# Normalising attention results in SBUF instead of fetching them back from DRAM

## The chip, the cores and the metric

The kernel runs on one core of a Trainium2 chip. The metric is the device time of one execution in microseconds (us). Five engines matter: TensorE (PE in the profile, with its weight loads as PEld), VectorE (DVE), ScalarE (ACT), GpSimd (POOL) and SyncE (SP), whose queue issues all of this kernel's transfers. The transfers themselves are carried by 16 DMA engines.

## The reference

Capped softmax attention, then two feed-forward blocks, all in float32 (the weights come as float64 words):

```python
B, H, S, D = 4, 12, 448, 64                       # q, k, v: (B, H, S, D)
scores = cap * np.tanh(q @ k.T / np.sqrt(D) / cap)
attn = np.exp(scores - scores.max(-1))
attn = attn / (attn.sum(-1) + 1e-09)
x = (attn @ v)        # reordered to 1792 tokens x 768
h = np.maximum(x @ w_in, 0.0)                     # 768 -> 2048
x = h * h @ w_out                                 # 2048 -> 768
gate = 1.0 / (1.0 + np.exp(-(x @ w_gate)))        # 768 -> 1536
return (gate * (x @ w_val)) @ w_out2              # 1536 -> 768
```

## The kernel before

**Tiling.** Two heads form a pair; there are 24 pairs (4 batches of 6), numbered n. The attention of a pair has four steps of 128 keys (the last one takes the 64 left of both heads at once). `scores` multiplies k by q, `softmax` applies tanh and exp on ACT, `pv` multiplies by v and accumulates in one PSUM tile "pv", of which there is one. Each v is stored beside 64 columns of ones, so that the result has, for head j of the pair, 64 rows of values and 64 rows that all hold the sum of the exponentials: for head 0 values in rows 0 to 63 and sums in 64 to 127, for head 1 the other way round. The first 12 pairs (`early`, batches 0 and 1) use float32 products; the other 12 split the operands in a high and a low part and take three products.

**Feed-forward.** The tokens are worked on in two passes: tokens 0 to 767 (blocks of 256 and 512), then 768 to 1791 (two blocks of 512). Every product there is taken three times, with high and low parts. A weight tile of the first pass is loaded as 64-bit words (`load_w`, line 480), converted on ACT and DVE (`convert`, lines 497 to 507), stored as float32 for the second pass (`keep`), and split (`round_w`, ACT and POOL). There are two tiles of words, two "raw" tiles and four split ones; a raw tile is free when its store has landed. The first pass has 82 weight tiles: 16 of w1, 24 of w2, 24 of the gate and its value, 18 of wo.

**Order of the work.** `Flow` plays the kernel through in the program's own model of time while it is built: jobs are generators that take a buffer (`"take"`), put an instruction into an engine's queue with a rank (lower goes first), or wait for a landing that `flow.landing` estimates. The order so found is fixed, and every engine then takes its instructions in that order, waiting where one isn't ready. `pick` writes PE's order: first the early pairs (the lead-in: scores of pair n between the products by v of pair n - 1), then the units of pass one, with the steps of the late pairs spread between them (`ATT`, `gap`), then pass two. The first units of pass one read all 768 features of a token, so the 256-token block needs pairs 0 to 5 and the 512-token block needs pairs 0 to 11.

**The stage that is changed.** `result` takes a pair from the end of its last `pv` step to x. Line 382 (early, DVE) or 384 (late, ACT) copies the PSUM tile into `xe`, one of 11 tiles "pt" of 128 x 2 x 448; the exponentials use the same tiles, and those of step 3 use three tiles "th" of 128 x 448. Line 390 stores 65 rows of each head (values and one row of sums) in DRAM, `xd`. Line 396 loads the two rows of sums as 16 rows of 56 (`sg`, by `dma`, line 222), lines 397 and 398 add eps and take the reciprocal on 16 partitions, line 399 stores the 896 reciprocals in `rd` (line 222 again). Line 410 fetches the values back from `xd`, 128 rows, and line 411 loads `rd` repeated over 64 rows for each head:

```python
y = xd[b][p].rearrange("(j r) s -> j r s", j=2)[:, 1:D + 1]
nc.sync.dma_start(out=xt[:, 0], in_=y)
nc.sync.dma_start(out=xt[:, 1], in_=rd[b][p].unsqueeze(1).to_broadcast((2, D, S)))
```

The target `xt` is a tile "acc" of the feed-forward part for early pairs and a tile "pt" for late ones. Line 415 multiplies on DVE, and `normalize` splits x in a high and a low part, which stay in SBUF (tokens below 768) or go to DRAM for pass two (`store_x`).

Of the kernel before, what the change touches and what calls it, by code (L numbers as in the profile page):

```python
# [10 lines left out]
F32 = mybir.dt.float32  # L11
# [3 lines left out]
ALU = mybir.AluOpType  # L15
ENGINES = mybir.EngineType

B, H, S, D = 4, 12, 448, 64
KC = 4
SP = 512  # L20
NP = H // 2
P = 128
DM = H * D
CC = DM // P
# [3 lines left out]
QK = S + SP  # L28
ALIGN = 256

PT, TH, WB = 11, 3, 4
# [122 lines left out]
def attn_mlp_kernel(ctx: ExitStack, tc: tile.TileContext, qk, v, cap, w1, w2, wg, wv, wo, out):  # L154
    nc = tc.nc
# [4 lines left out]
    dr = ctx.enter_context(tc.tile_pool(name="dr", bufs=1, space=bass.MemoryType.DRAM))  # L160
# [11 lines left out]
    def T(pool, tag, shape, dt=F32, bufs=1):  # L172
        pool = wp if pool == "wp" else open_pools[pool][1]
        return pool.tile(shape, dt, tag=tag, name=tag, bufs=bufs, align_bytes=ALIGN)

    def f32(ap):
        return ap.bitcast(F32)
# [8 lines left out]
    eps = const.tile([P, 1], F32, name="eps")  # L186
# [9 lines left out]
    def bank2(tag, pool=ps):  # L196
        return pool.tile([P, 2, 512], F32, tag=tag, name=tag, bufs=1)

    flow = Flow({
        "acc0": CC, "r0": 3, "g0": 2, "gx0": FG, "xa0": CC, "acc1": CC, "r1": 3, "g1": 2, "gx1": FG, "xa1": CC,  # L200
        "w64": 2, "raw": 2, "wh": WB, "pn": 0, "sb": 3, "pvb": 1, "v": 2, "qkh": 2, "pt": PT, "th": TH, "sg": 2,
        "qk": 2, "vr": 1})
# [5 lines left out]
    def on(engine, length, write, rank=1):  # L208
        return "on", engine, length, write, rank

    def act(out, in_, func=AF.Copy, rank=1, extra=0.0, **kw):
        return on("ACT", flow.act(cols(out)) + extra, lambda: nc.scalar.activation(out=out, in_=in_, func=func, **kw), rank)  # L212

    def sub(out, a, b, rank=1):
        return on("DVE", flow.dve(cols(out)), lambda: nc.vector.tensor_tensor(out=out, in0=a, in1=b, op=ALU.subtract), rank)  # L215

    def copy(out, in_, rank=1):
        return on("DVE", flow.dve1(cols(out)), lambda: nc.vector.tensor_copy(out, in_), rank)  # L218


    def dma(out, in_, size, store=False, rate=330e3, issue=0.42):
        yield on("SP", issue, lambda: nc.sync.dma_start(out=out, in_=in_))
        yield "for", flow.landing(size, store, rate)


# [3 lines left out]
    NV = 2  # L229
    v1, v2 = {}, {}  # L230

    XR = D + 2
    xd = [[dr.tile([2 * XR, S], F32, name=f"xd_{b}_{p}") for p in range(NP)] for b in range(B)]
    rd = [[dr.tile([2, S], F32, name=f"rd_{b}_{p}") for p in range(NP)] for b in range(B)]
    xn = [dr.tile([P, 2, WIDTH[1]], F32, name=f"xn_{p}") for p in range(NP)]
    RP, RN = 16, 2 * S // 16
# [5 lines left out]
    def early(n):  # L244
        return n < lead

    def score_tile(step, dt=F32):
        if step < 3:
            return T("att", "pt", [P, 2, S], dt, PT)
        return T("att", "th", [P, 1, S], dt, TH)  # L250
# [105 lines left out]
    def pv(n, step):  # L356
        if step == 0:
            st["o", n] = bank2("pv")
        o = st["o", n]
        ph, pl = st.pop(("p", n, step))  # L360
        c = (step + 1) % KC
        terms = [(v1, ph)] if early(n) else [(v2, ph), (v1, pl), (v1, ph)]
        for m, (vt, pt) in enumerate(terms):
            for j in range(2):

                r, u = (slice(0, P), j) if step < 3 else (slice(j * D, (j + 1) * D), 0)
                x = j if vt is v2 else 2 * j
                w = vt[n][r, c, x:x + 2, :].rearrange("p x d -> p (x d)")
                nc.tensor.matmul(  # L369
                    out=o[:, j, :S], lhsT=w, rhs=pt[r, u], start=step == 0 and m == 0, stop=step == 3 and m == len(terms) - 1)  # L370
        return result(n, step, o)

    def result(n, step, o):
        for _ in range(1 if early(n) else 2):
            flow.put("pt" if step < 3 else "th")
        if step < 3:
            return
        b, p = pairs[n]
        yield "take", "pt"
        xe = T("att", "pt", [P, 2, S], F32, PT)  # L380
        if early(n):
            yield on("DVE", 1.08, lambda: nc.vector.tensor_copy(xe, o[:, :, :S]), 0)
        else:
            yield act(xe, o[:, :, :S], rank=0)
        flow.put("pvb")
        flow.put("v")
        flow.fire(("pv", n))
        for j in range(2):
            r0, e0 = (XR, D - 1) if j else (1, 0)
            yield on("SP", 0.42, lambda: nc.sync.dma_start(out=xd[b][p][r0:r0 + D + 1], in_=xe[e0:e0 + D + 1, j]))  # L390
        yield "for", flow.landing(2 * (D + 1) * S * 4, True, 220e3)
        flow.put("pt")
        yield "take", "sg"
        sg = T("att", "sg", [RP, RN], bufs=2)
        rr = T("att", "rr", [RP, RN], bufs=2)
        yield from dma(sg, xd[b][p][XR - 1:XR + 1].rearrange("r (i s) -> (r i) s", s=RN), 0)
        yield on("DVE", 0.24, lambda: nc.vector.tensor_scalar(out=sg, in0=sg, scalar1=eps[:RP], scalar2=None, op0=ALU.add))
        yield on("DVE", 0.49, lambda: nc.vector.reciprocal(rr, sg))
        yield from dma(rd[b][p].rearrange("r (i s) -> (r i) s", s=RN), rr, 0, True)
        flow.put("sg")  # L400
        kind = "acc0" if early(n) else "pt"
        yield "take", kind
        if early(n):
            xt = T("mlp0", "acc", [P, QK], bufs=CC)[:, :2 * S].rearrange("p (x s) -> p x s", x=2)
        else:
            xt = T("att", "pt", [P, 2, S], F32, PT)
        y = xd[b][p].rearrange("(j r) s -> j r s", j=2)[:, 1:D + 1]

        def load():
            nc.sync.dma_start(out=xt[:, 0], in_=y)  # L410
            nc.sync.dma_start(out=xt[:, 1], in_=rd[b][p].unsqueeze(1).to_broadcast((2, D, S)))

        yield on("SP", 1.2, load, 0)
        yield "for", flow.landing(2 * P * S * 4, rate=170e3)
        yield on("DVE", flow.dve(S), lambda: nc.vector.tensor_tensor(out=xt[:, 0], in0=xt[:, 0], in1=xt[:, 1], op=ALU.mult), 0 if early(n) else 2)
        c0, c1 = b * S, (b + 1) * S
        for x0, x1 in ((c0, min(c1, T0)), (max(c0, T0), c1)):
            if x0 < x1:
                yield from normalize(n, x0, x1, xt[:, 0, x0 - c0:x1 - c0])
        flow.put(kind)  # L420

    def normalize(n, c0, c1, xu):
        p = pairs[n][1]
        w = c1 - c0
        if c1 <= T0:
            if ("x", 0, p) not in st:
                yield "take", "xa0"
                st["x", 0, p] = T("mlp0", "xa", [P, 2, WIDTH[0]], F32R, CC)  # L430
            dst = st["x", 0, p][:, :, c0:c1]
        else:
            yield "take", "pt"
            dst = T("att", "pt", [P, 2, S], F32R, PT)[:, :, :w]
        yield copy(dst[:, 0], xu, 0) if early(n) else act(dst[:, 0], xu, rank=2)
        yield sub(dst[:, 1], xu, f32(dst[:, 0]), 0 if early(n) else 2)
        if c1 <= T0:
            flow.fire(("x", 0, p, c1))
        else:
            flow.spawn(store_x(p, dst, c0 - T0, w))  # L440

    def store_x(p, dst, c, w):
        yield from dma(xn[p][:, :, c:c + w], f32(dst), 2 * P * w * 4, True)
        flow.put("pt")
        st["stored"] = st.get("stored", 0) + 1
        if st["stored"] == NP * 3:
            close_pool("att")
            open_pool("act1", "right")
            flow.fire("act1")
# [219 lines left out]
    for i, u in enumerate(units):  # L669
        k, kind, x = u["key"]  # L670
# [213 lines left out]
```

## Time and profile before

| | |
|---|---|
| median of 3 runs | 1340.55 us (1338.13 to 1343.11) |
| the profiled execution | 1339.74 us, span 1338.0 us from first to last instruction |
| PE busy | 1221.7 us (91%) |
| DVE busy | 645.7 us (48%) |
| ACT busy | 587.6 us (44%) |
| POOL busy | 278.8 us (21%) |
| DMA | 160.92 MB, 120 GB/s over the span |

A share over the whole span is a mean over unlike stages: the lead-in with the early pairs, pass one with the late pairs between its units, and pass two. They are better read by windows. PE's busy time holds time at a reduced clock as well: the granted clock (PEclk) is printed as a share of the full 2.4 GHz, and 0.50 is the lower level of 1.2 GHz. "Idle before" in a list in order of time is how long the engine stood still before that instruction, and behind the arrow stands what ended the wait. "SPq" rows are the issues of transfers; a transfer lands later.

### The profile page before, as it was taken

What the parts mean: (1) busy time and instruction counts of PE and PEld (TensorE: products, weight loads), DVE (VectorE), ACT (ScalarE), POOL (GpSimd) and SP (SyncE); (2) the same over time, 40 slices, a digit from 0 to 9 for tenths busy, and PEclk for the clock granted to TensorE, in tenths of its full rate; (3) what the DMA queues carried; (4) which work ended last, traced back from release to release, by engine and by line L of the source; (5) the groups of instructions that cost most, each with busy time, mean ns of one, the idle gap of its engine ahead of it and who ended that gap; (6) DMA issues with size and microseconds to landing.
All of it is one profiled execution on the core that took longest, in us unless ns stands there. A gap on an engine that the chain in (4) does not pass through costs nothing.

```text
span 1338.0 us, 15427 instructions
## 1 busy us (share of the span) xinstructions
PE 1221.7 (91%) x5880; PEld 984.8 (74%) x5880; DVE 645.7 (48%) x919; ACT 587.6 (44%) x866; POOL 278.8 (21%) x174
## 2 busy tenths in 40 slices
PE   8876737999899979988999999999999999999998
PEld 5443426888678767777778788888888888888887
DVE  3474425878688877687788520121215220122222
ACT  7664414565636665657555234424244223221220
POOL 0012001313122222122122222222222212212210
PEclk9887859999899999898999999999999999999999
DMA  5374323655555564655366751111211111111112
GB/s 170 108 221 139 122 81 121 192 176 164 181 163 180 151 191 154 187 188 162 117 177 190 254 196 52 44 54 41 64 39 56 55 32 55 56 32 58 53 33 102
DMA packets 76634, 160.92 MB, mean 120 GB/s; under 512 B 20448, under 2 KB 35088, under 8 KB 76560
## 3 DMA queue, kind: packets, MB, share of 16 engines
q1 hardware_dynamic: 76560, 159.93, 38.7%
q8 instruction: 46, 0.75, 0.2%
q14 instruction: 28, 0.23, 0.1%
HBM read 115.69 MB, written 44.21 MB: 120 GB/s over the span
## 4 chain that ended last, share of the span: by engine, by line
PE 51%; DMA 25%; DVE 13%; ACT 4%; issue 3%; SPq 2%; POOL 0%; ACTq 0%; DVEq 0%; POOLq 0%
PE pn L544 16%; PE pn L543 16%; PE pn L545 16%; DMA acc<-rd 6%; DMA pt<-rd 5%; DMA s_w<-raw 4%; DMA rd<-rr 3%; DMA s_wv<-raw 3%; DVE raw L505 2%; PE pv L369 2%; DVE raw L507 2%; DVE raw L501 2%; DMA s_wo<-raw 2%; DVE pt L215 1%; DMA xd<-pt 1%
## 5 line engine op out<-in xcount | busy, mean ns | idle before, releaser
L528 POOL TENSOR_TENSOR wl<-raw,wh 128x512 fp32r<-128x512 f32 (+1 forms) x164 | 276.0, 1684 | 1001.2 <-ACT wh L212 762.8
L543 PE MATMUL pn<-xa,wl 128*128 128x512 f32 (+1 forms) x960 | 353.0, 368 | 2.5 <-DVE g L588 1.3
L544 PE MATMUL pn<-xa,wh 128*128 128x512 f32 (+1 forms) x960 | 351.7, 366 | 0.0
L545 PE MATMUL pn<-xa,wh 128*128 128x512 f32 (+1 forms) x960 | 351.0, 366 | 0.0
L544 PE MATMUL pn<-gx,wh 128*128 128x512 f32 (+1 forms) x672 | 246.9, 367 | 4.9 <-DVE gx L215 4.8
L543 PE MATMUL pn<-gx,wl 128*128 128x512 f32 (+1 forms) x672 | 246.8, 367 | 4.8 <-ACT gx L212 4.7
L545 PE MATMUL pn<-gx,wh 128*128 128x512 f32 (+1 forms) x672 | 245.4, 365 | 0.0
L212 ACT ACTIVATE wh<-raw 128x512 fp32r<-128x512 f32 (+1 forms) x160 | 117.0, 731 | 284.6 <-PE pn L545 236.8
L543 PEld LDWEIGHTS pn<-xa,wl 128*128 128x128 f32 x960 | 183.7, 191 | 35.8 <-issue 3.9
L545 PEld LDWEIGHTS pn<-xa,wh 128*128 128x128 f32 x960 | 183.2, 191 | 29.0
L544 PEld LDWEIGHTS pn<-xa,wh 128*128 128x128 f32 x960 | 183.4, 191 | 28.8 <-DVE xa L215 0.3
L369 PE MATMUL pv<-pt,v 128*128 128x448 f32 x360 | 132.8, 503 | 77.3 <-DVE pt L218 38.5
L369 PEld LDWEIGHTS pv<-pt,v 128*128 128x128 f32 x360 | 70.9, 212 | 122.5 <-DVE pt L218 36.6
L215 DVE TENSOR_TENSOR gx<-g,gx 128x512 fp32r<-128x512 f32 (+1 forms) x112 | 83.8, 749 | 160.0 <-ACT gx L212 160.0
L543 PEld LDWEIGHTS pn<-gx,wl 128*128 128x128 f32 x672 | 128.4, 191 | 27.7 <-ACT gx L212 6.4
L544 PEld LDWEIGHTS pn<-gx,wh 128*128 128x128 f32 x672 | 128.3, 191 | 26.7 <-DVE gx L215 7.0
L545 PEld LDWEIGHTS pn<-gx,wh 128*128 128x128 f32 x672 | 128.3, 191 | 20.0
L606 DVE TENSOR_TENSOR acc<-pn,acc 128x512 f32<-128x512 f32 (+1 forms) x120 | 74.2, 620 | 122.4 <-PE pn L545 122.0
L588 DVE TENSOR_TENSOR g<-pn,r 128x512 f32<-128x512 f32 (+1 forms) x48 | 29.7, 619 | 176.5 <-PE pn L545 176.5
L212 ACT ACTIVATE raw<-w 128x512 f32<-128x512 f32 (+1 forms) x78 | 60.7, 778 | 114.4 <-DMA s_w<-raw 45.7
L212 ACT ACTIVATE gx<-g 128x512 fp32r<-128x512 f32 (+1 forms) x112 | 64.4, 575 | 68.9 <-DVE g L588 67.1
L212 ACT ACTIVATE r<-pn 128x512 f32<-128x512 f32 (+1 forms) x112 | 59.9, 535 | 69.6 <-PE pn L545 64.5
(72 smaller groups left out, 1042.5 us busy)
## 6 DMA issues: line engine op xcount, KB each, us to landing
w<-in_w_dram SPq DMA_DIRECT2D x16, 768.0 KB
w<-in_w_dram SPq DMA_DIRECT2D x24, 512.0 KB
w<-in_wg_dram SPq DMA_DIRECT2D x12, 768.0 KB
w<-in_wv_dram SPq DMA_DIRECT2D x12, 768.0 KB
w<-in_wo_dram SPq DMA_DIRECT2D x18, 512.0 KB
s_w<-raw SPq DMA_DIRECT2D x16, 384.0 KB
s_w<-raw SPq DMA_DIRECT2D x24, 256.0 KB
xa<-xn SPq DMA_DIRECT2D x12, 512.0 KB
```

What stands on the lines that cost most here:

```text
L212: return on("ACT", flow.act(cols(out)) + extra, lambda: nc.scalar.activation(out=out, in_=in_, func=func, **kw), rank)
L215: return on("DVE", flow.dve(cols(out)), lambda: nc.vector.tensor_tensor(out=out, in0=a, in1=b, op=ALU.subtract), rank)
L369: nc.tensor.matmul(out=o[:, j, :S], lhsT=w, rhs=pt[r, u], start=step == 0 and m == 0, stop=step == 3 and m == len(terms) - 1)
L501: yield on("DVE", flow.dve1(n), lambda: nc.vector.tensor_scalar(out=raw, in0=raw, scalar1=LOW, scalar2=HIGH, op0=ALU.max, op1=ALU.min))
L505: yield on("DVE", flow.dve(n), lambda: nc.vector.scalar_tensor_tensor(out=mu, in0=lo, scalar=29, in1=mu, op0=ALU.logical_shift_right, op1= ...
L507: yield on("DVE", flow.dve(n), lambda: nc.vector.scalar_tensor_tensor(out=mu, in0=hi, scalar=0xC0000000, in1=mu, op0=ALU.bitwise_and, op1= ...
L528: yield on("POOL", 0.15 + n * 0.0023, lambda: nc.gpsimd.tensor_tensor(out=lo, in0=raw, in1=f32(hi), op=ALU.subtract))
L543: nc.tensor.matmul(out=o, lhsT=wl[:, s], rhs=hi, start=i == 0, stop=False)
L544: nc.tensor.matmul(out=o, lhsT=wh[:, s], rhs=lo, start=False, stop=False)
L545: nc.tensor.matmul(out=o, lhsT=wh[:, s], rhs=hi, start=False, stop=i == n - 1)
L588: yield on("DVE", flow.dvep(w), lambda: nc.vector.tensor_tensor(out=g, in0=o, in1=st["r", k, f, off], op=ALU.mult))
L606: yield on("DVE", flow.dvep(w), lambda: nc.vector.tensor_tensor(out=acc, in0=o, in1=acc, op=ALU.add))
```

## The change

The values of a pair stay in `xe` until the reciprocals come. The DRAM tiles `xd` and both transfers to and from them are gone. Two transfers take the row of sums of each head from `xe` (one partition, 448 elements) to 8 partitions of 56 in `sg`, from SBUF to SBUF. The reciprocals still go to `rd` in DRAM and come back by two transfers, one for each head, of 64 rows each, into `bc`: a tile "acc" for early pairs, a tile "th" for late ones. Two multiplies, one for each half of the partitions, write into `xe[:, 0]`. `xe` is given back after `normalize`. The transfers, the addition and the reciprocal get rank 0, ahead of the others that are ready.

```diff
-    def dma(out, in_, size, store=False, rate=330e3, issue=0.42):
-        yield on("SP", issue, lambda: nc.sync.dma_start(out=out, in_=in_))
+    def dma(out, in_, size, store=False, rate=330e3, issue=0.42, rank=1):
+        yield on("SP", issue, lambda: nc.sync.dma_start(out=out, in_=in_), rank)
-    XR = D + 2
-    xd = [[dr.tile([2 * XR, S], F32, name=f"xd_{b}_{p}") for p in range(NP)] for b in range(B)]
-        for j in range(2):
-            r0, e0 = (XR, D - 1) if j else (1, 0)
-            yield on("SP", 0.42, lambda: nc.sync.dma_start(out=xd[b][p][r0:r0 + D + 1], in_=xe[e0:e0 + D + 1, j]))
-        yield "for", flow.landing(2 * (D + 1) * S * 4, True, 220e3)
-        flow.put("pt")
         yield "take", "sg"
         sg = T("att", "sg", [RP, RN], bufs=2)
         rr = T("att", "rr", [RP, RN], bufs=2)
-        yield from dma(sg, xd[b][p][XR - 1:XR + 1].rearrange("r (i s) -> (r i) s", s=RN), 0)
-        yield on("DVE", 0.24, lambda: nc.vector.tensor_scalar(out=sg, in0=sg, scalar1=eps[:RP], scalar2=None, op0=ALU.add))
-        yield on("DVE", 0.49, lambda: nc.vector.reciprocal(rr, sg))
-        yield from dma(rd[b][p].rearrange("r (i s) -> (r i) s", s=RN), rr, 0, True)
+        for j in range(2):
+            r0 = (1 - j) * D
+            src = xe[r0:r0 + 1, j].rearrange("o (i s) -> o i s", s=RN)
+            yield on("SP", 0.34, lambda: nc.sync.dma_start(out=sg[j * RP // 2:(j + 1) * RP // 2], in_=src), 0)
+        yield "for", flow.landing(0)
+        yield on("DVE", 0.24, lambda: nc.vector.tensor_scalar(out=sg, in0=sg, scalar1=eps[:RP], scalar2=None, op0=ALU.add), 0)
+        yield on("DVE", 0.49, lambda: nc.vector.reciprocal(rr, sg), 0)
+        yield from dma(rd[b][p].rearrange("r (i s) -> (r i) s", s=RN), rr, 0, True, rank=0)
         flow.put("sg")
-        kind = "acc0" if early(n) else "pt"
+        kind = "acc0" if early(n) else "th"
         yield "take", kind
-        if early(n):
-            xt = T("mlp0", "acc", [P, QK], bufs=CC)[:, :2 * S].rearrange("p (x s) -> p x s", x=2)
-        else:
-            xt = T("att", "pt", [P, 2, S], F32, PT)
-        y = xd[b][p].rearrange("(j r) s -> j r s", j=2)[:, 1:D + 1]
-        def load():
-            nc.sync.dma_start(out=xt[:, 0], in_=y)
-            nc.sync.dma_start(out=xt[:, 1], in_=rd[b][p].unsqueeze(1).to_broadcast((2, D, S)))
-        yield on("SP", 1.2, load, 0)
-        yield "for", flow.landing(2 * P * S * 4, rate=170e3)
-        yield on("DVE", flow.dve(S), lambda: nc.vector.tensor_tensor(out=xt[:, 0], in0=xt[:, 0], in1=xt[:, 1], op=ALU.mult), 0 if early(n) else 2)
+        bc = T("mlp0", "acc", [P, QK], bufs=CC)[:, :S] if early(n) else score_tile(3)[:, 0]
+        for j in range(2):
+            yield on("SP", 0.42, lambda: nc.sync.dma_start(
+                out=bc[j * D:(j + 1) * D], in_=rd[b][p][j].unsqueeze(0).to_broadcast((D, S))), 0)
+        yield "for", flow.landing(P * S * 4, rate=135e3)
+        xu = xe[:, 0]
+        for j in (1, 0):
+            r = slice(j * D, (j + 1) * D)
+            yield on("DVE", flow.dve(S), lambda: nc.vector.tensor_tensor(
+                out=xu[r], in0=xe[r, j], in1=bc[r], op=ALU.mult), 0 if early(n) else 2)
+        flow.put(kind)
         c0, c1 = b * S, (b + 1) * S
         for x0, x1 in ((c0, min(c1, T0)), (max(c0, T0), c1)):
             if x0 < x1:
-                yield from normalize(n, x0, x1, xt[:, 0, x0 - c0:x1 - c0])
-        flow.put(kind)
+                yield from normalize(n, x0, x1, xu[:, x0 - c0:x1 - c0])
+        flow.put("pt")
```

## Rows read from the trace of the kernel before

**Rows 1.** Busy time of each engine by stage, with granted clock and DMA share.

```profile
core 0: us, PE busy (x) PEld busy (x) DVE busy (x) ACT busy (x) POOL busy (x), PEclk, DMA share, GB/s
0.00:100.00 100.00, 78.56 (x336) 46.65 (x337) 50.03 (x72) 67.00 (x81) 5.14 (x8) 0.93 0.55 167
100.00:230.00 130.00, 82.41 (x349) 55.42 (x348) 56.76 (x108) 46.30 (x70) 14.40 (x10) 0.76 0.37 115
230.00:767.00 537.00, 493.81 (x2685) 413.15 (x2686) 414.29 (x582) 308.47 (x455) 130.36 (x74) 0.96 0.57 175
767.00:1338.00 571.00, 566.91 (x2513) 469.56 (x2511) 124.60 (x158) 165.78 (x262) 128.89 (x83) 1.00 0.20 62
```

**Rows 2.** The chain of waits, shares of the span by line.

```profile
by line: PE pn L544 16.1%; PE pn L543 16.0%; PE pn L545 15.9%; DMA acc<-rd 6.3%; DMA pt<-rd 4.7%; DMA s_w<-raw 3.7%; issue 3.1%; DMA rd<-rr 2.8%; DMA s_wv<-raw 2.6%; DVE raw L505 2.3%; PE pv L369 2.2%; DVE raw L507 1.8%; DVE raw L501 1.7%; 
```

**Rows 3.** PE in order of time: start, length, instruction, idle before and what released it.

```profile
129.40 3.33 PE L369 MATMUL pv<-pt,v 128*128 128x448 f32 x4 [11.93 <-DVE xa L215]
...
196.84 1.78 PE L369 MATMUL pv<-th,v 64*128 64x448 f32 x6 [6.38 <-DVE th L218]
```

**Rows 4.** Who DVE waited for, 0 to 230, then 230 to 767: total, times, longest.

```profile
DVE acc L415 <- DMA acc<-rd: 69.3, 11, 8.8
...
DVE pt L415 <- DMA pt<-rd: 50.4, 10, 7.9
```

**Rows 5.** Busy time by window, 167 to 173 (columns as in rows 1).

```profile
167.00:173.00 6.00, 0.00 (x0) 0.00 (x0) 0.00 (x0) 0.88 (x1) 0.00 (x0) 0.50 0.13 51
```

**Rows 6.** The DMA queue of SP in order of time: start, length of the issue, transfer.

```profile
30.92 0.31 SPq L222 DMA_DIRECT2D rd<-rr  x1
...
33.74 0.53 SPq L411 DMA_DIRECT2D acc<-rd  x1
...
105.23 4.45 SPq L410 DMA_DIRECT2D acc<-xd  x1
```

**Rows 7.** DVE in order of time: evacuations (line 382) and multiplies (line 415).

```profile
20.01 1.09 DVE L382 COPY pt<-pv 128x896 f32<-128x896 f32 x1 [2.14 <-PE pv L369]
...
28.10 1.09 DVE L382 COPY pt<-pv 128x896 f32<-128x896 f32 x1 [2.14 <-PE pv L369]
...
45.55 0.62 DVE L415 TENSOR_TENSOR acc<-acc 128x448 f32<-128x448 f32 x1 [3.35 <-DMA acc<-rd]
...
157.36 1.08 DVE L382 COPY pt<-pv 128x896 f32<-128x896 f32 x1
...
203.95 0.63 DVE L415 TENSOR_TENSOR acc<-acc 128x448 f32<-128x448 f32 x1 [6.50 <-DMA acc<-rd]
```

**Rows 8.** One pair's store, sums and reciprocal: SP's queue, then DVE, in order of time.

```profile
206.61 0.95 SPq L390 DMA_DIRECT2D xd<-pt  x2
209.48 0.31 SPq L222 DMA_DIRECT2D sg<-xd  x1
...
210.94 0.24 DVE L397 TENSOR_SCALAR sg<-sg,eps 16x56 f32<-16x56 f32 x1 [2.87 <-DMA sg<-xd]
211.21 0.49 DVE L398 RECIPROCAL rr<-sg 16x56 f32<-16x56 f32 x1
```

**Rows 9.** Pieces of the chain of waits: start, length, what (a weight's store landing).

```profile
265.23 4.61 DMA s_w<-raw
...
290.51 11.47 DMA s_w<-raw
```

**Rows 10.** Busy time by window, 20 to 36 (columns as in rows 1).

```profile
20.00:36.00 16.00, 16.00 (x76) 9.44 (x74) 6.46 (x8) 14.88 (x19) 0.00 (x0) 1.00 0.47 127
```

**Rows 11.** PE in order of time, after 205 (columns as in rows 3).

```profile
227.84 0.50 PE L544 MATMUL pn<-gx,wh 128*128 128x512 f32 x1 [2.66 <-DVE gx L215]
...
747.88 0.50 PE L543 MATMUL pn<-xa,wl 128*128 128x512 f32 x1 [1.25 <-DVE g L588]
```

**Rows 12.** SP's queue: the eighth and the ninth load of a weight.

```profile
148.96 0.38 SPq L480 DMA_DIRECT2D w<-in_w_dram  x1
...
216.25 2.11 SPq L480 DMA_DIRECT2D w<-in_w_dram  x1
```

## The prediction

> **What bounds the kernel now.** I read four views in this order: busy time by stage, the chain of waits, then the order of time on TensorE (PE), VectorE (DVE) and the DMA queue. By stage the reader is to see where PE, the engine with the most work, is not working: 21.4 us idle of the first 100, 47.6 of the next 130, 43.2 of the 537 that follow, 4.1 of the last 571 [rows 1]. The first two stages also ran at a mean granted clock of 0.93 and 0.76. So half of what can be won lies in the first 230 us, and the last 571 us have nothing to give.
>
> The chain of waits names the place: the load of the reciprocals ("acc<-rd" for early pairs, "pt<-rd" for late ones) holds 6.3% and 4.7% of the span, 147 us [rows 2]. In PE's order of time, five gaps, the first ended at 129.40 and the last at 196.84, sum to 41.4 us, every one released by DVE [rows 3]. DVE itself waited 69.3 us in the first 230 us for "acc<-rd" and 50.4 us later for "pt<-rd", both at line 415, the multiply [rows 4]. DVE takes its instructions in order, so behind that multiply stand the next pair's evacuation and the exponentials' rounding, for which PE waits.
>
> Why is the load slow? In a stretch with nothing else in flight the DMA engines are busy 0.13 of their time, which is two of 16, and move 51 GB/s [rows 5]. A pair's two loads (line 410 fetches 224 KB back, line 411 224 KB of reciprocals, both with a leading dimension of 2) are 459 KB: 9.0 us at that rate. The broadcast issued at 33.74 is waited for until 45.55 [rows 6, 7], and when a second pair's loads come behind, the issue itself takes 4.45 us [rows 6], as if the queue were full, and weights, v and q/k queue behind it. This is a backlog on two engines, not a shortage of bandwidth.
>
> **Part 1: the pair's chain.** Before, from the end of a pair's evacuation to its multiply: 45.55 - 21.10 = 24.5 us for pair 0, and 203.95 - 158.44 = 45.5 us for pair 11 [rows 7]. The change drops two stores (line 390), the fetch back (line 410) and their landings. What is left, step by step:
> - Two sum transfers. Issue 2 x 0.31 [rows 8] = 0.6 us. The trace has no SBUF-to-SBUF transfer; the nearest row is the same 16 rows of 224 B from DRAM, issued at 209.48 and used at 210.94: 1.5 us [rows 8]. The source is now one partition, so between 0 and twice that (2.9 us); I take 1.5.
> - Addition and reciprocal: 0.24 + 0.49 = 0.7 us [rows 8]. Store of the reciprocals, from its issue at 30.92 to the next issue that needs it at 33.74: 2.8 us [rows 6].
> - Two broadcasts of 64 rows. Issue 2 x 0.5 [rows 6] = 1.0 us. Landing: unknown. The nearest row is the old store of 130 rows of the same 1792 B, 1.9 us from its last issue's end (207.56) to 209.48 [rows 8] (over 100 GB/s). The other end is two engines as now: 229 KB at 51 GB/s is 4.5 us, with 1.9 of latency 6.4. I take 3.0, nearer the low end because 64 rows are divided on both sides.
>
> Sum 9.6 us; with waiting in SP's order (its queue holds weight and v loads between these steps) I take 12, bounds 10 and 17. Then two multiplies of 64 partitions. No DVE row of before is of that height: each costs 0.31 us if time goes by all elements, 0.62 as the full one [rows 7] if it goes by elements per partition; I take 0.62, so a pair costs DVE 0.62 us more than before.
>
> **Part 2: the first 205 us.** Undisturbed, pairs follow each other every 8.09 us (evacuations at 20.01 and 28.10), with PE busy 16.0 of the 16 us from 20 to 36 [rows 7, 10]: PE itself is the bound there. Before, the twelfth evacuation came at 157.36, 12.5 us a pair [rows 7]. After: five periods of 8.1 and, since from then on weight conversion also sits on DVE, six of 9.5 (estimate, bounds 8.1 and 11): 20 + 40.5 + 57 = 117.5. Then 1.1 us for the evacuation, 12 for the chain, 2 for multiplies and rounding: the first product over all 12 pairs has its operands at 133, where before it was 205 (the twelfth multiply began at 203.95 [rows 7], its rounding follows). The late steps that PE did meanwhile in its gaps won't all fit: I add 4, 137. As a check: PE's work in the first 230 us is 78.6 us at 0.93 and 82.4 at 0.76 [rows 1], 136 us at full clock, so at most 94 us can be won there. Part 2 is worth 205 - 137 = 68 us, bounds 52 (periods of 11, a chain of 17) and 80 (8.1 and 10).
>
> **Part 3: from 205 to 767.** Seventeen PE gaps end in the few us behind such a multiply, 28.8 us in all, from 2.66 us before 227.84 to 1.25 us before 747.88 [rows 11]. The low clock behind the gaps costs some 9 us more: 0.04 of 494 busy us is 20 [rows 1], and I count half of it to these gaps. A weight's store that was issued right behind the broadcast landed after 11.47 us, another after 4.61 [rows 9]; that goes too. At most 38 us to win. Against it:
> - DVE gets 12 x 0.62 = 7.5 us of multiplies; hidden by 123 idle us of 537 [rows 1]. Uncovered they cost 7.5.
> - The result's tile (one of 11) is held through the chain, and a late pair takes one of 3 "th" tiles for the reciprocals. Its multiply has DVE's lowest priority; the next pair's step 3, which needs that tile, comes some 45 us later (12 pairs in the 537 us of [rows 1]). Hidden, at nothing; if the hold were over 45 us, PE would wait the excess once a pair. Of the early pairs' 11 tiles six hold exponentials and five are left for results, which covers a chain of 5 x 8.1 = 40 us.
> - SP: five transfers a pair in place of six, at the head of the queue. The wait for the reciprocals' landing now stands ahead of both loads instead of one; queued behind it are weight loads, 2.8 us each time [rows 6], which the two buffered weights cover.
> - Head start: by 149 us eight weights had been loaded, the next only at 216 [rows 12], so PE started with full buffers. At 137 it will have fewer. The other 74 of the 82 weights of the first pass take the 537 us of [rows 1], 7.3 us each; up to three fewer are 22 us.
>
> I take +10 for this part, bounds -22 and +38. Nothing after 767 changes.
>
> **A rule against the change.** The two broadcasts go to disjoint halves of the partitions. The Trainium skill, page "DMA: Bandwidth & Descriptors", section "Rules for kernel authors", says of this "Don't bother — they serialize" and asks for one transfer of 128 partitions. By that rule the halves as such are worth nothing, which is the second rival. The same section says that a leading broadcast dimension of c copies confines a transfer to at most c engines; the 0.13 of [rows 5] agrees with that for c = 2.
>
> **The rivals.**
> - *Weights take over* (16%). With the loads gone, the weight conversion (raw buffers, its DVE work, its store) paces the stage after 137. For it: in some stretches the chain of waits already runs through that store [rows 9]. Against: PE was busy 92% of that stage. Then part 3 costs 22 in place of winning 10: 1262 + 32 = 1294.
> - *Halves bring nothing* (13%). The broadcast stays on two engines: 6.4 in place of 3.0 us. Each chain gates the next pair but one: 11/2 x 3.4 + 3.4 = 22 us: 1284. For it: no such transfer stands in the trace. Against: the store in [rows 8], of as many rows of the same length, ran at twice that rate.
> - *No gain* (4%). What is won early is lost to a replanned order, within 0.5% of 1340.
> - *Slower: DVE becomes the bound* (5%). One mechanism: the second multiply of each pair lies on DVE's path in both stages, 24 x 0.62 = 15 us: 1355. It decides if the broadcasts land as late as now (over 24 us behind the evacuation), so that nothing is won early, and DVE's idle time is no cover. Against: 120 of DVE's idle us are the very wait that is removed [rows 4].
>
> **How the numbers follow.** Forecast (62%): span 1338.0 - 68 - 10 = 1260; the profiled execution took 1339.74, 1.74 more than its span, so 1262. Its time is 0.8 us below the median of the runs shown (1340.55), nothing beside the range. Both high bounds together would give 1222, both low ones 1310; as they hardly come together, its own range is 1232 to 1290. The range reaches over the first two rivals: 1232 to 1302; no gain, slower, and some 8% beyond the ends are left out. A measurement of this kernel can tell about 0.5% (6.7 us) from no change. Faster 0.91, same 0.04, slower 0.05.
>
> **What would show it.** Evacuations at line 382 every 8 to 10 us up to the twelfth near 118; DVE's wait at the multiply falling from 120 us to under 40; the first 512-wide product near 130 to 140; no issue of over 2 us on the broadcast's line; granted clock in 100 to 230 near 0.95. The forecast is wrong if the twelfth evacuation still comes after 140 (chain not shortened, or DVE too full), or if PE's idle time from there to the last pass exceeds the 43 us of now (weights).

## The result, and the profile after

| | before | after |
|---|---|---|
| median | 1340.07 us | 1229.76 us (1224.96 to 1231.51) |
| ratio | | 0.9169, 95% interval 0.9137 to 0.9201 |
| span of the profiled execution | 1338.0 us | 1228.7 us |
| PE busy | 1221.7 us | 1190.2 us |
| DVE busy | 645.7 us | 651.9 us |
| bytes moved | 160.92 MB | 149.81 MB |

The change saved 110 us where 78 were forecast. The time lies 2 us below the low end of the range.

Busy time by stage of the changed kernel, with the columns of [rows 1]:

```profile
0.00:100.00 100.00, 92.94 (x423) 56.44 (x424) 69.87 (x113) 80.89 (x98) 7.04 (x8) 1.00 0.55 164
100.00:230.00 130.00, 119.35 (x652) 98.31 (x651) 101.34 (x162) 78.09 (x129) 33.66 (x22) 0.95 0.56 166
230.00:658.00 428.00, 410.84 (x2297) 349.17 (x2296) 356.39 (x512) 261.86 (x378) 111.73 (x62) 0.98 0.59 183
658.00:1228.70 570.70, 567.07 (x2513) 469.68 (x2512) 124.31 (x158) 165.99 (x262) 129.09 (x83) 1.00 0.19 59
```

PE's idle time in the first two stages is 7.1 and 10.7 us, where [rows 1] had 21.4 and 47.6; in the third it is 17.2 for 43.2. The granted clock of 100 to 230 is 0.95 for 0.76.

The chain of waits of the changed kernel, for [rows 2], and all that is left of [rows 4], the waits of DVE for the reciprocals:

```profile
by line: PE pn L538 18.1%; PE pn L539 18.0%; PE pn L540 18.0%; DMA s_wg<-raw 1.1%; DMA s_wv<-raw 0.9%; DVE raw L500 0.9%; PE pv L365 0.7%; DVE raw L502 0.7%; issue 0.6%; ACT pt L212 0.4%; ACT raw L212 0.4%; PE se L321 0.4%; DVE raw L496 0.4
```

```profile
DVE pt L408 <- DMA acc<-rd: 2.5, 1, 2.5
```

"acc<-rd" and "pt<-rd" held 11% of the chain; neither loads of that name nor "th<-rd", their new name for late pairs, are among its larger parts now. Over the whole span DVE waited 126.2 us for them (69.3 and, as the line of before below says, 56.9; the second window of [rows 4] leaves one late wait out), and now 2.5, once.

```profile
DVE pt L415 <- DMA pt<-rd: 56.9, 11, 7.9
```

DVE in order of time, for [rows 7]: the first two evacuations, the first pair's multiplies, the twelfth evacuation and its pair's first multiply:

```profile
20.34 1.09 DVE L378 COPY pt<-pv 128x896 f32<-128x896 f32 x1 [2.14 <-PE pv L365]
...
28.48 1.09 DVE L378 COPY pt<-pv 128x896 f32<-128x896 f32 x1 [1.47 <-PE pv L365]
...
34.89 1.27 DVE L408 TENSOR_TENSOR pt<-pt,acc 64x448 f32<-64x448 f32 x2
...
109.59 1.09 DVE L378 COPY pt<-pv 128x896 f32<-128x896 f32 x1 [1.78 <-PE pv L365]
...
125.75 0.62 DVE L408 TENSOR_TENSOR pt<-pt,acc 64x448 f32<-64x448 f32 x1 [2.45 <-DMA acc<-rd]
```

Evacuations follow each other every 8.1 us up to the last (20.34 to 109.59, eleven periods). From an evacuation's end to its multiply it is 34.89 - 21.43 = 13.5 us for pair 0 and 125.75 - 110.68 = 15.1 us for pair 11, where it was 24.5 and 45.5; over the twelve early pairs it is 12.3 to 17.1 us. The DMA issues of the broadcasts (line 402) and of the sums (line 392), shortest, median and longest in ns:

```profile
L402 SPq DMA_DIRECT2D acc<-rd x24: 448/492/925, 30.4 to 119.4; - x24
L392 SPq DMA_DIRECT2D sg<-pt x48: 641/687/807, 21.5 to 614.0; - x48
```

No broadcast took over 0.93 us to issue; before, the longest took 4.41, and the fetch back in [rows 6] 4.45.

### The profile page after: what moved, and what is told of

Same layout as the page of the kernel before. It is cut to its first block, busy times and chain, and to the rows that moved or that the text cites. A ratio compares the mean times of both kernels' runs of the same rounds, so it can differ in the third digit from the quotient of the medians.

```text
span 1228.7 us, 15417 instructions
## 1 busy us (share of the span) xinstructions
PE 1190.2 (97%) x5880; PEld 973.6 (79%) x5880; DVE 651.9 (53%) x943; ACT 586.8 (48%) x866; POOL 281.5 (23%) x174
## 2 busy tenths in 40 slices
DMA packets 70489, 149.81 MB, mean 122 GB/s; under 512 B 20496, under 2 KB 28944, under 8 KB 70416
## 4 chain that ended last, share of the span: by engine, by line
PE 55%; DVE 3%; DMA 2%; ACT 1%; issue 1%; SPq 0%; ACTq 0%
PE pn L538 18%; PE pn L539 18%; PE pn L540 18%; DMA s_wg<-raw 1%; DMA s_wv<-raw 1%; DVE raw L500 1%; PE pv L365 1%; DVE raw L502 1%; ACT pt L212 0%; ACT raw L212 0%; PE se L321 0%; DVE raw L496 0%; DVE raw L498 0%; ACT L212 0%; DVE pt L215 0%
## 5 line engine op out<-in xcount | busy, mean ns | idle before, releaser
L523 POOL TENSOR_TENSOR wl<-raw,wh 128x512 fp32r<-128x512 f32 (+1 forms) x164 | 278.8, 1701 | 916.7 <-ACT wh L212 715.1
L215 DVE TENSOR_TENSOR gx<-g,gx 128x512 fp32r<-128x512 f32 (+1 forms) x112 | 87.5, 782 | 165.2 <-ACT gx L212 165.0
L365 PE MATMUL pv<-pt,v 128*128 128x448 f32 x360 | 116.9, 459 | 12.8 <-DVE pt L218 7.0
L365 PEld LDWEIGHTS pv<-pt,v 128*128 128x128 f32 x360 | 66.7, 195 | 48.5 <-issue 24.2
```

The lines of the kernel that those rows point to most:

```text
L365: nc.tensor.matmul(out=o[:, j, :S], lhsT=w, rhs=pt[r, u], start=step == 0 and m == 0, stop=step == 3 and m == len(terms) - 1)
L523: yield on("POOL", 0.15 + n * 0.0023, lambda: nc.gpsimd.tensor_tensor(out=lo, in0=raw, in1=f32(hi), op=ALU.subtract))
```

## The experiments

To compare runs, each span is cut at two events that every kernel has: the start of the first 512-wide product, with which the first work begins that needs all 12 early pairs (the twelfth only for the last of its six groups of features), and the issue of the first output. First the kernel before, then the change (columns of [rows 1]):

```profile
0.00:198.50 198.50, 134.80 (x567) 81.42 (x567) 91.37 (x154) 99.14 (x126) 13.53 (x14) 0.82 0.46 141
198.50:757.80 559.30, 511.02 (x2756) 426.41 (x2754) 424.54 (x597) 320.43 (x475) 134.52 (x76) 0.95 0.55 168
757.80:1338.00 580.20, 575.86 (x2561) 476.95 (x2559) 129.77 (x168) 167.98 (x266) 130.74 (x84) 1.00 0.21 67
```

```profile
0.00:134.50 134.50, 117.15 (x546) 73.79 (x547) 97.81 (x166) 95.46 (x120) 14.27 (x14) 0.95 0.54 158
134.50:647.10 512.60, 495.07 (x2762) 420.49 (x2761) 424.51 (x610) 323.46 (x481) 136.29 (x76) 0.98 0.58 179
647.10:1228.70 581.60, 577.97 (x2576) 479.33 (x2575) 129.60 (x168) 167.92 (x265) 130.96 (x85) 1.00 0.20 63
```

The first part fell by 64.0 us, the second by 46.7, and the third grew by 1.4. In the second TensorE's instruction counts agree within 0.3%, and PE's idle time fell from 48.3 to 17.5 us (-30.8), its busy time from 511.0 to 495.1 (-15.9) at a clock of 0.98 for 0.95. My sum had 68 for the first part and 10 for the second, so the second is what had to be explained.

The first theory, "two engines": both loads of a pair have a leading dimension of 2 and so run on two DMA engines, and everything queued behind them is late. The rival, "fewer steps": the gain comes from what the change leaves out (stores, fetch, bytes).

**Both loads split by head, nothing else changed.**

```diff
-            nc.sync.dma_start(out=xt[:, 0], in_=y)
-            nc.sync.dma_start(out=xt[:, 1], in_=rd[b][p].unsqueeze(1).to_broadcast((2, D, S)))
+            for j in range(2):
+                nc.sync.dma_start(out=xt[j * D:(j + 1) * D, 0], in_=y[j])
+            for j in range(2):
+                nc.sync.dma_start(out=xt[j * D:(j + 1) * D, 1], in_=rd[b][p][j].unsqueeze(0).to_broadcast((D, S)))
```

> The kernel before with both loads split by head: the values' fetch back and the reciprocals each come by two transfers of 64 rows. No step is left out, as many bytes move, the sums still go through DRAM. Theory 'two engines': nearly the whole gain, 1235 to 1260 us, DVE's wait at the multiply under 30 us, no issue over 2 us at the loads. Theory 'fewer steps': over 1310 us.

Measured: 1218.75 us, ratio 0.9104 (0.9073 to 0.9135), 16 us below the forecast of "two engines". It keeps every step, moves the 160.92 MB of before, leaves the order of the work as it was, and is faster than the change. DVE's waits for the reciprocals, and the three parts of the span:

```profile
DVE acc L417 <- DMA acc<-rd: 6.4, 5, 2.1
...
DVE pt L417 <- DMA pt<-rd: 2.6, 3, 1.5
```

```profile
0.00:135.80 135.80, 121.81 (x567) 75.86 (x567) 91.10 (x154) 98.67 (x126) 16.89 (x14) 0.97 0.69 208
135.80:635.70 499.90, 488.01 (x2746) 414.15 (x2745) 425.00 (x597) 320.85 (x475) 139.32 (x76) 0.99 0.63 188
635.70:1216.70 581.00, 577.37 (x2571) 478.72 (x2570) 129.56 (x168) 168.02 (x266) 130.80 (x85) 1.00 0.21 66
```

The waits are 9 us in place of 126, and PE's idle time in the second part is 11.9 us. "Fewer steps" is out: leaving the steps out is not needed for any of the gain.

**Only the reciprocals split** (of the diff above, the edit of `xt[:, 1]` alone):

> The kernel before with one edit: the reciprocals come by two transfers of 64 rows, one a head, in place of one transfer with a leading dimension of 2; the fetch back of the values stays as it was. Theory 'two engines': half of the 459 KB leaves the two engines, the other half (229 KB, 4.5 us at 51 GB/s) stays on them, so a pair's chain falls from 24 to some 18 us and the backlog goes: 1270 to 1300 us, DVE's wait at the multiply falls from 126 to 40 to 70 us. Theory 'fewer steps' (the gain comes from leaving out stores and fetch, the halves bring nothing): 1330 to 1340 us, the wait unchanged.

Measured: 1252.25 us, ratio 0.9343 (0.9319 to 0.9367), 18 us less than the forecast's low end. DVE's waits:

```profile
DVE acc L416 <- DMA acc<-rd: 32.3, 10, 5.4
...
DVE pt L416 <- DMA pt<-rd: 15.5, 7, 4.1
```

They sum to 47.8 us, within the forecast's 40 to 70.

**Only the values' fetch back split** (the edit of `xt[:, 0]` alone):

> The kernel before with only the values' fetch back split by head; the reciprocals still come by one transfer with a leading dimension of 2. It tells a slow broadcast (64 reads of one row) from a slow leading dimension. Theory 'two engines, whatever they read': the mirror of the run that split the reciprocals alone (1252 us), 1245 to 1262 us. Theory 'the broadcast is the slow one': 1300 us or more.

Measured: 1275.29 us, ratio 0.9527 (0.951 to 0.9544), 13 us above "two engines", far below "the broadcast is the slow one". DVE's waits:

```profile
DVE acc L416 <- DMA acc<-rd: 28.9, 8, 5.7
DVE pt L416 <- DMA pt<-rd: 25.8, 7, 5.0
```

Either half of the bytes taken off the two engines brings more than half the gain (87 and 64 of 121 us). The backlog is smaller then, but not gone: the waits are 47.8 and 54.7 us where they were 126.2, and the longest issue among the pairs' transfers is still 3.84 and 3.24 us. The values' fetch back is the cheaper one to leave on the two engines. It also holds them for less time: in the packet records of the two traces exactly two packets of 1792 bytes (a row of these transfers) are in flight for 81 us with the fetch left there and for 112 us with the broadcast left. The place in the chain (the fetch is issued before the reciprocals' wait, the broadcast comes last) may be another reason; no run tells them apart.

**The change with one transfer for the reciprocals**, issued in the first turn of the loop over heads:

```diff
-            yield on("SP", 0.42, lambda: nc.sync.dma_start(
-                out=bc[j * D:(j + 1) * D], in_=rd[b][p][j].unsqueeze(0).to_broadcast((D, S))), 0)
+            yield on("SP", 0.42, lambda: None if j else nc.sync.dma_start(
+                out=bc, in_=rd[b][p].unsqueeze(1).to_broadcast((2, D, S))), 0)
```

> The changed kernel with one edit: the reciprocals come by one transfer with a leading dimension of 2 (as before the change) in place of two of 64 rows. Theory 'two engines': 229 KB on two engines, 4.5 us a pair longer than the spread ones; by the prediction's working 22 us on the early pairs (11/2 x 3.4 + 3.4) and some more on the late ones: 1248 to 1270 us. Theory 'halves as such bring nothing': 1225 to 1235 us, as the change.

Measured: 1285.39 us, ratio 0.9597 (0.9576 to 0.9618), 15 us above the forecast of "two engines": the two transfers of 64 rows are worth 55.6 us of the change's 110. Its first two parts, and DVE's waits:

```profile
0.00:172.30 172.30, 128.60 (x546) 78.86 (x547) 97.76 (x166) 96.48 (x120) 14.23 (x14) 0.88 0.41 124
172.30:702.00 529.70, 500.12 (x2764) 421.95 (x2764) 424.28 (x609) 322.77 (x481) 135.82 (x76) 0.97 0.57 171
```

```profile
DVE pt L408 <- DMA acc<-rd: 19.9, 7, 4.2
...
DVE pt L408 <- DMA th<-rd: 14.9, 7, 4.5
```

This run leaves the fetch back out, and the one above (1275.29 us) splits it, both with the broadcast as one transfer: the kernel that leaves it out is not the faster one.

The packet records of the traces show the two engines themselves. In the first part the packets of 1792 bytes of these two kernels are the rows of the broadcasts and nothing else. As one transfer, the 128 rows of a pair take 4.7 to 6.7 us (median 5.8) from the first packet to the end of the last, with exactly two packets in flight for 83% of that time and never over four. As two transfers of 64 rows they take 1.6 to 4.2 us (median 2.2), with three or more in flight for 83% of the time and six on average.

Against the change 37.8 us are lost in the first part and 17.1 in the second. "Halves as such bring nothing" is out, with the mechanism right and the price wrong: the forecast had 22 us for it, on the early pairs alone.

**The change for early pairs only, and for late pairs only.** The other pairs go through the old stage; the second kernel has `not early(n)` in this line.

```diff
+        yield from (tail_new if early(n) else tail_old)(n, xe)
```

> The changed stage for the first 12 pairs only; the late 12 pairs use the old one. It tells apart where the 47 us between the first 512-wide product and the first output come from, of which the sum had 10. Theory 'each part has its own loads': the 64 us up to the first 512-wide product are won, the 47 behind it are not: 1270 to 1282 us. Theory 'the early part alone' (the later part was late only from a bad start): 1230 to 1245 us.

> The changed stage for the last 12 pairs only; the first 12 use the old one. Theory 'each part has its own loads': 1340 - 47 = 1288 to 1300 us, with the first 512-wide product still near 200 us. Theory 'the early part alone': 1325 to 1340 us.

Measured: 1269.06 us, ratio 0.9472 (0.9451 to 0.9494), and 1293.89 us, ratio 0.9665 (0.9633 to 0.9697). The first two parts of each, early first:

```profile
0.00:132.80 132.80, 117.31 (x546) 73.81 (x547) 99.04 (x166) 95.44 (x120) 13.90 (x14) 0.96 0.55 160
132.80:686.80 554.00, 510.76 (x2777) 427.81 (x2775) 418.18 (x597) 323.65 (x481) 133.25 (x76) 0.96 0.56 172
```

```profile
0.00:200.40 200.40, 135.91 (x567) 82.50 (x567) 91.52 (x154) 99.21 (x126) 13.55 (x14) 0.82 0.46 140
200.40:717.00 516.60, 493.79 (x2741) 417.47 (x2740) 429.31 (x610) 318.95 (x475) 138.69 (x76) 0.98 0.58 175
```

The two gains, 70.5 and 45.6 us, add up to 116 for the 110 of both. With the early pairs alone the first part is 132.8 us, as short as the change's, and the second 554.0, nearly the 559.3 of before. With the late pairs alone it is the other way round: 200.4 and 516.6. (The profiled execution with the late pairs alone took 1300.58 us, 6.7 above the median of its runs.) So the 47 us of the second part were the late pairs' own loads, and no consequence of a better start.

**Why is the change 10 us slower than the split loads?** Both once more, side by side:

> The kernel with both loads split by head once more, beside the change on the same chip, to give their difference with an interval: 1215 to 1222 us.

> The changed kernel once more, beside the run above: 1226 to 1233 us, 0.6 to 1.2% slower than it. If the two overlap, the 11 us are not to be explained.

Measured: 1218.15 us, ratio 0.9102 (0.908 to 0.9123), and 1228.21 us, ratio 0.9177 (0.9156 to 0.9199). The intervals don't meet. The theories: the doubled multiply, the ranks, and a late start of the weights.

```diff
-        yield on("DVE", flow.dve(S), lambda: nc.vector.tensor_tensor(out=xt[:, 0], in0=xt[:, 0], in1=xt[:, 1], op=ALU.mult), 0 if early(n) else 2)
+        for j in (1, 0):
+            r = slice(j * D, (j + 1) * D)
+            yield on("DVE", flow.dve(S), lambda: nc.vector.tensor_tensor(out=xt[r, 0], in0=xt[r, 0], in1=xt[r, 1], op=ALU.mult), 0 if early(n) else 2)
```

> The faster experiment (both loads split by head, 1219 us) with its one multiply of 128 partitions replaced by two of 64, as the change has them; nothing else. Theory 'the doubled multiply': DVE gets 24 x 0.62 = 15 us more and the weights are converted later in the lead-in: 1226 to 1233 us, so that it explains the 11 us by which the change is slower. Theory 'order, ranks and held tiles': 1217 to 1222 us.

Measured, for the split loads with two multiplies: 1224.14 us, ratio 0.9141 (0.9123 to 0.916), between the two. Its first two parts:

```profile
0.00:135.60 135.60, 121.54 (x567) 75.31 (x567) 96.58 (x165) 98.62 (x126) 14.41 (x14) 0.96 0.70 208
135.60:643.80 508.20, 492.66 (x2754) 416.91 (x2753) 437.30 (x611) 319.11 (x475) 146.41 (x76) 0.99 0.61 185
```

The second part is 508.2 us for 499.9 with one multiply and 512.6 in the change. So the doubled multiply explains about half of the difference (5.4 us by the medians, 6.8 by the whole spans of the traces), with intervals that touch.

The change with the old ranks:

> The changed kernel with the ranks of the sums' transfers, the addition, the reciprocal and its store at 1, as before the change. Theory 'ranks matter': the chain waits behind weight loads and conversions again, 1233 to 1245 us; or, if rank 0 held the weights up in the lead-in, 1218 to 1225 us. Theory 'the doubled multiply' has nothing for the ranks: 1226 to 1233 us.

Measured: 1229.44 us, ratio 0.9183 (0.9157 to 0.9209). The ranks are worth nothing here.

The change, then the split loads, with the weights' loading begun after pair 3 (`WSTART` 3 for 5):

> The changed kernel with the weights' loading begun after pair 3 in place of pair 5 (one constant). Theory 'head start': the 7.2 us that PE waited at 130 us for a converted weight go, and the low clock behind them: 1217 to 1224 us. Theory 'DVE is full in the lead-in': earlier weights push the pairs' own DVE work back, 1229 to 1240 us.

> The kernel with both loads split by head and the same earlier weights. It never waited for a converted weight in the lead-in, so by 'head start' it is unchanged, 1215 to 1222 us; by 'DVE is full' 1222 to 1230 us.

Measured: 1221.83 us, ratio 0.9133 (0.9112 to 0.9155), and 1217.98 us, ratio 0.9099 (0.9077 to 0.9121). In the change PE stood still once for a converted weight, 7.16 us, and then ran at a granted clock of 0.50 up to the first 512-wide product; PE in order of time, and the stretch from 100 to 135 without and with the earlier weights:

```profile
130.56 0.58 PE L538 MATMUL pn<-xa,wl 128*128 128x256 f32 x1 [7.16 <-POOL wl L523]
...
134.57 0.53 PE L538 MATMUL pn<-xa,wl 128*128 128x512 f32 x1
```

```profile
100.00:135.00 35.00, 24.71 (x127) 17.81 (x126) 27.93 (x53) 14.76 (x24) 7.24 (x6) 0.80 0.50 145
```

```profile
100.00:135.00 35.00, 30.86 (x160) 23.16 (x159) 26.70 (x56) 17.64 (x30) 2.93 (x5) 0.95 0.48 142
```

PE's idle time there falls from 10.3 to 4.1 us and the clock rises from 0.80 to 0.95. This is a real cost of the change (6.4 us by the medians). It lies in the first part, where the change looks no slower than the split loads (134.5 and 135.8 us). But the two parts don't hold the same work: the change has 546 TensorE products in its first part and the split loads have 567, so 21 products of the late pairs come behind the cut in the change (2762 and 2576 products in its other two parts, for 2746 and 2571). With the earlier weights the change's first part, with the same 546 products, is 126.1 us. The two costs, 5.4 and 6.4 us, add up to the difference of 10 us and a little more, and with the earlier weights in both kernels 3.9 us are left, with intervals that overlap, no more than the doubled multiply costs by itself. So nothing need be left over; no run has both edits at once, and the longer hold of the tiles was not tried by itself.

The fastest version is the kernel of before with both loads split by head: 1218 us, 0.8% below the change.

## Why the prediction was wrong

*What bounds the kernel:* right. The place (line 411's load, DVE's wait at line 415, PE behind DVE) and the cause (a backlog on two engines, not bandwidth) were read from [rows 2 to 6], and the run with both loads split shows them without any other edit.

*Part 1, the chain:* 12 us forecast, 13.5 and 15.1 measured for the first and the last pair, 12.3 to 17.1 over the twelve, so within its bounds but for 0.1 us. The multiply of 64 partitions took 0.62 us, as the one of 128: time goes by elements per partition, and the doubled cost that I chose was right. The sums' transfers cost more than the 1.5 us and 2 x 0.31 of issue: their issue alone is 0.69 us each, and for pair 0 it is 26.26 - 21.43 = 4.8 us from the evacuation's end to the addition where the sum had 2.1.

```profile
26.26 0.23 DVE L394 TENSOR_SCALAR sg<-sg,eps 16x56 f32<-16x56 f32 x1
```

But my working gave the dropped stores and fetch a share of the gain; the run with all of them kept says that the gain needs none of it.

*Part 2, the first part of the span:* 68 forecast, 64 measured by the cut above. The forecast's own mark was a later one, the first product that needs the twelfth pair; before and after it began at

```profile
204.99 0.49 PE L543 MATMUL pn<-xa,wl 128*128 128x512 f32 x1 [1.21 <-DVE xa L218]
...
138.11 0.39 PE L538 MATMUL pn<-xa,wl 128*128 128x512 f32 x1
```

66.9 us apart. That this is so near is partly luck: two errors nearly cancel. The evacuations came every 8.1 us throughout, not 9.5 from the sixth on (8 us better), and PE then waited for a converted weight and ran at the lower clock (the head start, which I had put into part 3). The bounds of 52 and 80 were a little too wide: the steps named for them give 54 and 78.

*Part 3, the step that failed:* 10 forecast, 46.7 measured, or 43.8 from the forecast's own mark; both lie beyond its high bound of 38. I had found 28.8 us of PE gaps behind the late multiplies and 9 of clock, half of the clock's loss of 20, then took 10 as a compromise with a head start of up to 22. Measured: 30.8 us less idle time and 15.9 less busy time at the higher clock (29.6 and 14.3 from the own mark). So the gaps were sized right, the clock's loss was worth some 5 to 7 us more than the half that I counted, and the head start was no cost of this stage: it came in the first part, and the run with earlier weights puts it at 6.4 us. The mechanism was right; the term was mis-sized by netting it against a cost whose rows [rows 12] lie ahead of this stage.

*The rivals:* "weights take over" did not come; PE is busy 97% of the second part. "Halves bring nothing" fell, at a price of 55.6 us and not 22. The Trainium skill's page "DMA: Bandwidth & Descriptors" says in "Rules for kernel authors" that two transfers to disjoint halves serialize and that one should be used. This does not hold here, where the one transfer has a leading dimension of 2 (median 5.8 us a pair for one, 2.2 for two); the measurement decides. The same page of the Trainium skill says, in "Why a DMA increments its semaphore by 16 and not by 1", that a transfer gets the largest number of engines, up to 16, that divides the slowest dimension of its source and of its target. By that rule it is 2 for the old loads and 16 for 64 rows. The traces agree for 2 (two packets in flight, and the share of 0.13 in [rows 5]); for 64 rows they show six packets in flight on average, and not the number of engines itself. "Slower: DVE becomes the bound" named a real cost, about 5 to 7 us of the 15 it gave, and no more than that.

## What to carry to other kernels

When a load of some 200 KB takes 10 us while the DMA share stands near 0.13, look at the outermost dimension of its pattern before anything else; two lines that split it by that dimension were worth more than a new data path. Try the smallest edit that tests the cause first: here it kept every step and was the fastest. And a gain read from gaps in one stage should not be netted against a cost that no row of that stage shows.

## What the runs showed of the hardware that was not expected

The issue of a transfer of 448 elements from one partition to eight took 0.64 to 0.81 us on SP (48 of them), where the same sums from DRAM took 0.31 [rows 8]. And a late transfer costs more than the wait that carries its name. The run with one transfer for the reciprocals lost 54.9 us against the change in its first two parts. DVE's waits for the reciprocals grew from 2.5 to 34.8 us (19.9 and 14.9), and its waits for the sums from 9.2 to 26.5; the change's line stands first:

```profile
DVE sg L394 <- DMA sg<-pt: 9.2, 5, 3.1
...
DVE sg L394 <- DMA sg<-pt: 26.5, 10, 5.4
```

On PE 38.4 of the 54.9 us are idle time; the other 16.5 are busy time at a lower clock, 0.88 and 0.97 in the two parts where the change had 0.95 and 0.98.
